# Exponential per head on ScalarE, and the PSUM banks dealt out anew, in chunk attention with a gated and a plain MLP

## The chip, the cores and the metric

The kernel runs on one core of a Trainium2 chip. The metric is the time of one execution on the device in microseconds; the time of a kernel is the median of several runs.

## The reference

Three parts follow one another, all in float32, for 8 batches of 576 rows of 512 numbers (8 heads of 64).

```python
scores = scale * np.matmul(q_c, k_c.transpose(0, 1, 2, 4, 3))   # chunks of 64 rows, each against itself
scores = scores - np.max(scores, axis=-1, keepdims=True)
attn = np.exp(scores)
attn = attn / (np.sum(attn, axis=-1, keepdims=True) + 1e-09)
out = np.matmul(attn, v_c)
...
gate = 1.0 / (1.0 + np.exp(-gate_pre))        # gate_pre: causal convolution of out with 5 taps
x = (gate * (out @ w_val)) @ w_out
...
xn = (x - mu) / np.sqrt(var + 1e-06) * g_ln
result = x + np.maximum(xn @ w_ch1, 0.0) @ w_ch2
```

## The kernel before, in words

The 4608 rows are cut into 18 **units** of 256 rows and 9 **blocks** of 512 rows, so two units make a block. Three stages follow one another.

*Attention and gate.* `slot(u)` writes the program of a unit. `a3(u)` multiplies queries by keys into the PSUM tile `sc` (two banks: 2 x 8 x 64 columns), VectorE takes the maximum of each 64 scores (L167) and subtracts it while it copies `sc` to the SBUF tile `ex` (L170), ScalarE takes the exponential of the whole `ex`, 1024 columns, in place (L174), VectorE sums (L176), inverts (L177) and scales into `pr` (L179). `a4(u)` turns `pr` on TensorE into the PSUM tile `pst` (L186, two banks) and ScalarE copies it to `pT` (L188). `a5(u)` multiplies by the values into the PSUM tile `x` (L219, two banks); ScalarE copies `x` to `xf` (L233) and, rounded, to `xh` (L236), VectorE keeps the rest in `xl` (L238). `a4` and `a5` run one unit behind `a3` (`LAG`). For each block, `conv` (L248 on ScalarE, four times L250 on VectorE per slice, into `cg`), `sigm` (L257) and four `val` chains of 12 matmuls (`psv`, L264) make the gated product: VectorE reads `psv` times `cg` into `gv` (L282), ScalarE rounds it to `gh` (L285), VectorE keeps the rest in `gl` (L286). Four `proj` chains of 12 matmuls (`pso`, also L264) follow, which ScalarE copies out (L299) and stores (L300). Between these, `split` decodes the 64-bit weights of the later stages (L87 to L90, L95, L96).

*First block of the plain MLP* (`ff1`, `ff2`), then *the other eight blocks*, two at a time (`ff_pair`).

The 8 PSUM banks of the first stage are: two for chains (pool `ps_d`, one bank a tile), two for `sc`, two for `x`, two for `pst` (pool `ps_p`).

A tile scheduler orders the instructions of each engine when the kernel is built, from dependences, priorities and costs; `tc.high_priority()` moves a group ahead. TensorE's order follows the source where `manual_schedule` is open: up to unit 4 (`MANUAL`), and again from the MLP on. Each engine then runs its list in order and waits for semaphores, and the SyncE queue holds the loads.

```python
kt, qt = t[:, 0], t[:, 1]
sc = ps_s.tile([P, 2, NG, CH], F32, tag="sc", name="sc")
```

Of the kernel before, what the change touches and what calls it, by code (L numbers as in the profile page):

```python
# [8 lines left out]
F32 = mybir.dt.float32  # L9
F32R = mybir.dt.float32r  # L10
U32 = mybir.dt.uint32
ACTF = mybir.ActivationFunctionType
ALU = mybir.AluOpType
AX = mybir.AxisListType
PSUM = bass.MemoryType.PSUM
# [4 lines left out]
def tile_chunk_attention_gated_mlp(ctx: ExitStack, tc: tile.TileContext, qk, v, w_val, conv_w, w_out, g_ln, w1, w2, out):  # L20
    nc = tc.nc
    B, S, DM = out.shape
# [39 lines left out]
    pA = s_a.enter_context(tc.tile_pool(name="pA", bufs=2, side="right"))  # L62
    ps_s = s_a.enter_context(tc.tile_pool(name="ps_s", bufs=1, space=PSUM))
    ps_x = s_a.enter_context(tc.tile_pool(name="ps_x", bufs=1, space=PSUM))
    ps_p = s_a.enter_context(tc.tile_pool(name="ps_p", bufs=1, space=PSUM))

    a_dram = [dram.tile([P, DM], F32, name=f"ad{f}") for f in range(NF)]
    w1c = [dram.tile([P, 2, 2, 2 * P], F32, name=f"wc{i}") for i in range(NF * 7 // 4)]
# [83 lines left out]
    def a3(u):  # L152
        t = qkr.pop(u)
        kt, qt = t[:, 0], t[:, 1]
        sc = ps_s.tile([P, 2, NG, CH], F32, tag="sc", name="sc")
        for g in range(NG):
            n, hp = divmod(g, NP)
            for c in range(2):
                cs = slice(n * P + c * CH, n * P + (c + 1) * CH)
                for par in range(2):  # L160
                    r0 = CH * par
                    nc.tensor.matmul(
                        out=sc[CH * c:CH * c + CH, par, g, :], lhsT=qt[r0:r0 + CH, hp, cs], rhs=kt[r0:r0 + CH, hp, cs],
                        start=True, stop=True,
                    )
        mx = pA.tile([P, 2, NG], F32, tag="mx", name="mx")
        nc.vector.tensor_reduce(out=mx, in_=sc, op=ALU.max, axis=AX.X)  # L167
        whole = exps[u % len(exps)]
        ex = whole[:, :, :, 0:CH]
        nc.vector.tensor_tensor(  # L170
            out=ex.rearrange("p g r k -> p r g k"), in0=sc,
            in1=mx.unsqueeze(3).to_broadcast([P, 2, NG, CH]), op=ALU.subtract,
        )
        nc.scalar.activation(out=ex, in_=ex, func=ACTF.Exp, scale=scale)  # L174
        sm = pA.tile([P, NG, 2], F32, tag="sm", name="sm")
        nc.vector.tensor_reduce(out=sm, in_=whole, op=ALU.add, axis=AX.X)  # L176
        nc.vector.reciprocal(out=sm, in_=sm)  # L177
        pr = pt[u] = pA.tile([P, NG, 2, CH], F32, tag="pr", name="pr")
        nc.vector.tensor_tensor(out=pr, in0=ex, in1=sm.unsqueeze(3).to_broadcast([P, NG, 2, CH]), op=ALU.mult)  # L179

    def a4(u):
        pr = pt.pop(u)
        t = pA.tile([P, NG, P], F32, tag="pT", name="pT", bufs=1)
        ps = ps_p.tile([P, NG, P], F32, tag="p", name="pst")
        for g in range(NG):
            nc.tensor.transpose(out=ps[:, g, :], in_=pr[:, g].rearrange("p r k -> p (r k)"), identity=ident)  # L186
        with tc.high_priority():
            nc.scalar.activation(out=t, in_=ps, func=ACTF.Copy)  # L188
            pT[u] = t
# [71 lines left out]
    def chain(ps, ops):  # L261
        n = len(ops)
        for i, (lt, rh) in enumerate(ops):
            nc.tensor.matmul(out=ps, lhsT=lt, rhs=rh, start=(i == 0), stop=(i == n - 1))  # L264

    def val(j, f):
        hs, ls = wv["vs"]
        fs = slice(f * P, (f + 1) * P)
        if j == NB - 1:
            ps = p2["acc"].tile([P, BLK], F32, tag=f"acc{f}", name="psv")  # L270
        else:
            ps = ps_d.tile([P, BLK], F32, tag="d", name="psv")
        ops = []
        for c in range(CT):
            ops += [(hs[c][:, fs], xh[j][:, c, :]), (hs[c][:, fs], xl[j][:, c, :]), (ls[c][:, fs], xh[j][:, c, :])]
        chain(ps, ops)
        o = boundary(j)
        gv = pD2.tile([P, BLK], F32, tag="gv", name="gv")
        with tc.high_priority():
            for lo, hi, sh in ((0, o, 0), (o, BLK, HALO)):  # L280
                if lo < hi:
                    nc.vector.tensor_tensor(out=gv[:, lo:hi], in0=ps[:, lo:hi], in1=cg[:, f, lo + sh:hi + sh], op=ALU.mult)  # L282
            a = pD1.tile([P, BLK], F32R, tag=f"gh{f}", name="gh")
            b = pD1.tile([P, BLK], F32R, tag=f"gl{f}", name="gl")
            nc.scalar.activation(out=a, in_=gv, func=ACTF.Copy)  # L285
            nc.vector.tensor_tensor(out=b, in0=gv, in1=a, op=ALU.subtract)  # L286
        gh[j, f], gl[j, f] = a, b

    def proj(j, t):
        hs, ls = wv["os"]  # L290
        ts = slice(t * P, (t + 1) * P)
        ps = ps_d.tile([P, DM], F32, tag="d", name="pso")
        ops = []
        for f in range(CT):
            ops += [(gh[j, f][:, ts], hs[f]), (gh[j, f][:, ts], ls[f]), (gl[j, f][:, ts], hs[f])]
        chain(ps, ops)
        y = pD2.tile([P, DM], F32, tag="y", name="y")
        with tc.high_priority():
            nc.scalar.activation(out=y, in_=ps, func=ACTF.Copy)  # L299
            nc.scalar.dma_start(out=y_dram[j][ts, :], in_=y)  # L300
# [343 lines left out]
    def taps():  # L644
        cwr = stg.tile([KC * CT, P], F32, tag="da", bufs=3, name="cwr")
        decode(cwu, cwr)
        ps = ps_p.tile([P, NP * P], F32, tag="p", name="pst")
        nc.tensor.transpose(out=ps[:, 0:KC * CT], in_=cwr, identity=ident[0:KC * CT, 0:KC * CT])
        nc.tensor.transpose(out=ps[:, KC * CT:(KC + 1) * CT], in_=gr, identity=ident[0:CT, 0:CT])
        nc.vector.tensor_copy(out=cw, in_=ps[:, 0:(KC + 1) * CT])  # L650
# [150 lines left out]
```

## Time and profile before

| | us |
|---|---|
| median of three runs | 1138.32 (1137.65 to 1139.07) |
| the profiled execution, its own time | 1135.95 |
| its span in the trace | 1134.2 |
| time around the span | 1.75 |
| busy: TensorE / VectorE / ScalarE / GpSimd | 1070.5 / 712.8 / 483.5 / 110.6 |
| mean granted TensorE clock | 0.977 of full speed |

The page gives busy time of each engine over the whole span; the stages differ, so the rows further down are read by stretch. A matmul's recorded duration overlaps its successor's, so for TensorE the distance from start to start counts, not the busy time. The attention and gate stage lies between 0 and about 345 us, the first MLP block up to about 455 us.

### The profile page before, as it was taken

What the parts mean: (1) busy time and instruction counts of PE and PEld (TensorE: products, weight loads), DVE (VectorE), ACT (ScalarE), POOL (GpSimd) and SP (SyncE); (2) the same over time, 40 slices, a digit from 0 to 9 for tenths busy, and PEclk for the clock granted to TensorE, in tenths of its full rate; (3) what the DMA queues carried; (4) which work ended last, traced back from release to release, by engine and by line L of the source; (5) the groups of instructions that cost most, each with busy time, mean ns of one, the idle gap of its engine ahead of it and who ended that gap; (6) DMA issues with size and microseconds to landing.
All of it is one profiled execution on the core that took longest, in us unless ns stands there. A gap on an engine that the chain in (4) does not pass through costs nothing.

```text
span 1134.2 us, 17091 instructions
## 1 busy us (share of the span) xinstructions
PE 1070.5 (94%) x6862; PEld 871.4 (77%) x6862; DVE 712.8 (63%) x1171; ACT 483.5 (43%) x832; POOL 110.6 (10%) x120
## 2 busy tenths in 40 slices
PE   5788989899898989899999999999999999999998
PEld 5676767777786868688888888888888888878877
DVE  6999999888967877545647434447444437432434
ACT  3566666566574754434444123333223333221221
POOL 2021001000003443322210000000000000000000
PEclk9799999999999999999999999999999999999999
DMA  8535546531135753634342733332733222622212
GB/s 334 169 121 166 187 133 213 179 107 72 46 120 188 225 165 119 236 118 145 126 141 100 232 99 106 112 106 89 232 105 103 99 93 89 227 93 93 75 38 75
DMA packets 58581, 155.28 MB, mean 137 GB/s; under 512 B 5742, under 2 KB 13958, under 8 KB 56198
## 3 DMA queue, kind: packets, MB, share of 16 engines
q1 hardware_dynamic: 53318, 144.75, 37.7%
q10 hardware_dynamic: 5184, 9.44, 2.2%
q8 instruction: 54, 0.88, 0.3%
q14 instruction: 25, 0.20, 0.1%
HBM read 116.41 MB, written 37.75 MB: 136 GB/s over the span
## 4 chain that ended last, share of the span: by engine, by line
PE 65%; DVE 24%; issue 4%; ACT 3%; DMA 3%; POOL 0%; SPq 0%; ACTq 0%; POOLq 0%; DVEq 0%
PE acc L499 16%; PE x L525 15%; PE psf L499 14%; PE zy L525 10%; DVE cg L250 7%; PE psv L264 5%; DVE da L89 2%; DVE da L90 2%; DVE sm L176 2%; PE acc L385 1%; DVE xl L238 1%; DMA raw<-in_moe_w_ch 1%; DVE h L537 1%; PE psh L264 1%; DVE mx L167 1%
## 5 line engine op out<-in xcount | busy, mean ns | idle before, releaser
L545 DVE TENSOR_TENSOR c<-x,c 128x512 f32<-128x512 f32 x96 | 66.2, 690 | 237.3 <-ACT c L541 181.1
L499 PE MATMUL psf<-w,h 128*128 128x512 f32 x768 | 186.0, 391 | 0.0
L499 PE MATMUL acc<-w,h 128*128 128x512 f32 x768 | 186.0, 391 | 0.0
L499 PEld LDWEIGHTS acc<-w,h 128*128 128x128 f32 x768 | 144.2, 188 | 31.4
L499 PEld LDWEIGHTS psf<-w,h 128*128 128x128 f32 x768 | 144.2, 188 | 31.4
L525 PE MATMUL x<-t,wc 128*128 128x512 f32 x576 | 148.2, 393 | 3.4 <-DVE c L545 3.4
L541 ACT ACTIVATE c<-zy 128x512 f32<-128x512 f32 x96 | 58.0, 604 | 188.4 <-PE zy L525 188.3
L525 PEld LDWEIGHTS x<-t,wc 128*128 128x128 f32 x576 | 108.8, 189 | 27.8 <-DVE c L545 4.6
L536 ACT ACTIVATE h<-c 128x512 fp32r<-128x512 f32 x96 | 60.5, 631 | 136.1 <-DVE c L545 135.5
L250 DVE SCALAR_TENSOR_TENSOR cg<-xf,cw,cg 128x516 f32<-128x516 f32 (+1 forms) x176 | 108.6, 661 | 0.0
L504 DVE TENSOR_TENSOR yt<-psf,yt 128x512 f32<-128x512 f32 x128 | 88.2, 691 | 25.0 <-PE psf L499 21.1
L525 PE MATMUL zy<-b,wc 128*128 128x512 f32 x384 | 98.9, 393 | 0.0
L525 PEld LDWEIGHTS zy<-b,wc 128*128 128x128 f32 x384 | 71.2, 188 | 14.6
L537 DVE SCALAR_TENSOR_TENSOR h<-c,h 128x512 fp32r<-128x512 f32 x96 | 68.5, 713 | 14.0 <-ACT h L536 13.9
L264 PE MATMUL psv<-xh,vh 128*128 128x512 f32 x144 | 62.1, 432 | 15.5 <-DVE gv L282 15.5
L96 POOL TENSOR_TENSOR w<-da,w 128x512 fp32r<-128x512 f32 x32 | 48.6, 1526 | 128.8 <-ACT w L95 125.6
L264 PE MATMUL psv<-xh,vl 128*128 128x512 f32 x144 | 59.6, 414 | 0.0
L264 PE MATMUL psv<-xl,vh 128*128 128x512 f32 x144 | 59.6, 414 | 0.0
L264 PE MATMUL pso<-oh,gh 128*128 128x512 f32 x144 | 58.5, 406 | 0.1
L264 PE MATMUL pso<-oh,gl 128*128 128x512 f32 x144 | 56.5, 393 | 0.4 <-DVE gl L286 0.4
L264 PE MATMUL pso<-ol,gh 128*128 128x512 f32 x144 | 56.1, 390 | 0.0
L393 POOL TENSOR_TENSOR wc<-raws,wc 128x256 fp32r<-128x256 f32 x56 | 45.3, 831 | 107.4 <-ACT wc L392 100.5
(108 smaller groups left out, 1563.3 us busy)
## 6 DMA issues: line engine op xcount, KB each, us to landing
wc<-wc SPq DMA_DIRECT2D x112, 512.0 KB, 3.2
qkr<-in_qk SPq DMA_DIRECT2D x18, 1024.0 KB, 5.9
raw<-in_moe_w_ch SPq DMA_DIRECT2D x32, 512.0 KB, 4.2
vr<-in_v SPq DMA_DIRECT2D x18, 512.0 KB, 4.2
yd<-y ACTq DMA_DIRECT2D x36, 256.0 KB, 2.8
out<-yt SPq DMA_DIRECT2D x36, 256.0 KB, 3.7
yr<-yd SPq DMA_DIRECT2D x32, 256.0 KB, 3.2
yt<-yd SPq DMA_DIRECT2D x32, 256.0 KB, 4.1
```

The lines of the kernel that those rows point to most:

```text
L89: nc.vector.scalar_tensor_tensor(out=au, in0=hw, scalar=0x80000000, in1=au, op0=ALU.bitwise_and, op1=ALU.bitwise_or)
L96: nc.gpsimd.tensor_tensor(out=lo, in0=a, in1=hi, op=ALU.subtract)
L250: nc.vector.scalar_tensor_tensor(out=o, in0=x[:, f, i + lo:i + hi], scalar=cw[:, i * CT + f:i * CT + f + 1], in1=o, op0=ALU.mult, op1=ALU.add,
L264: nc.tensor.matmul(out=ps, lhsT=lt, rhs=rh, start=(i == 0), stop=(i == n - 1))
L393: eng.tensor_tensor(out=lo, in0=a, in1=hi, op=ALU.subtract)
L499: nc.tensor.matmul(out=ps, lhsT=lt, rhs=rh, start=(g == 0 and k == 0 and (first or half)), stop=(g == 1 and k == 2 and (last or half)),)
L504: nc.vector.tensor_tensor(out=yt[i], in0=ps, in1=yt[i], op=ALU.add)
L525: nc.tensor.matmul(out=ps, lhsT=lt, rhs=rh, start=(start and c == 0 and i == 0), stop=(c == 1 and i == 2), skip_group_check=True)
L536: nc.scalar.activation(out=t[:, 0, :], in_=src, func=ACTF.Relu)
L537: nc.vector.scalar_tensor_tensor(out=t[:, 1, :], in0=src, scalar=0.0, in1=t[:, 0, :], op0=ALU.max, op1=ALU.subtract)
L541: nc.scalar.activation(out=t, in_=zy, func=ACTF.Copy)
L545: nc.vector.tensor_tensor(out=t, in0=x, in1=t, op=ALU.add)
```

## The change

Four things are edited.

1. In `a3`, VectorE no longer subtracts the maximum. It multiplies the small tile `mx` (16 numbers a partition) by `-scale`, and ScalarE reads `sc` from PSUM in 16 instructions of 64 columns, each with its column of `mx` as bias, and writes `ex`. The sum, the inverse and the product on VectorE stay. `sc` is now read until the last of the 16 exponentials, where it was read until the subtraction.
2. `pst` and `x` share one PSUM tile (tag `x`, two banks, one buffer).
3. The two banks so freed are the pool `ps_e` (two buffers of one bank). The chains of `val` and `proj` take a bank from `ps_d` and from `ps_e` by turns, through `ps_chain`, until the stage is closed; so four chains have banks.
4. The transposed taps use a tile of `ps_e`.

```diff
-    ps_p = s_a.enter_context(tc.tile_pool(name="ps_p", bufs=1, space=PSUM))
+    ps_e = s_a.enter_context(tc.tile_pool(name="ps_e", bufs=2, space=PSUM))
...
-        nc.vector.tensor_tensor(
-            out=ex.rearrange("p g r k -> p r g k"), in0=sc,
-            in1=mx.unsqueeze(3).to_broadcast([P, 2, NG, CH]), op=ALU.subtract,
-        )
-        nc.scalar.activation(out=ex, in_=ex, func=ACTF.Exp, scale=scale)
+        nc.vector.tensor_scalar(out=mx, in0=mx, scalar1=-scale, scalar2=None, op0=ALU.mult)
+        for r in range(2):
+            for g in range(NG):
+                nc.scalar.activation(out=ex[:, g, r, :], in_=sc[:, r, g, :], func=ACTF.Exp, scale=scale, bias=mx[:, r, g:g + 1])
...
-        ps = ps_p.tile([P, NG, P], F32, tag="p", name="pst")
+        ps = ps_x.tile([P, NG, P], F32, tag="x", name="pst")
...
+    chains = 0
+
+    def ps_chain(name):
+        nonlocal chains
+        chains += 1
+        pool = ps_d if chains % 2 or "acc" in p2 else ps_e
+        return pool.tile([P, BLK], F32, tag="d", name=name)
+
...
-            ps = ps_d.tile([P, BLK], F32, tag="d", name="psv")
+            ps = ps_chain("psv")
...
-        ps = ps_d.tile([P, DM], F32, tag="d", name="pso")
+        ps = ps_chain("pso")
...
-        ps = ps_p.tile([P, NP * P], F32, tag="p", name="pst")
+        ps = ps_e.tile([P, BLK], F32, tag="d", name="pst")
```

The scheduler makes another order of it. The first place is ScalarE's list in the first unit of block 3, from the turned probabilities to the copies of `x`. `ex_143` is one of the two `ex` buffers, `da` a decoded weight, and lines after the edit are seven higher in the later functions and one lower in `a3` to `a5`. Before:

```order
L188 ACTIVATE pT<-pst 128x1024
L285 ACTIVATE gh<-gv 128x512
L174 ACT_TABLE_LOAD
L174 ACTIVATE ex_143<-ex_143 128x16x64
L285 ACTIVATE gh<-gv 128x512
L87 ACTIVATE da<-raw_3785 128x512
L233 ACTIVATE xf<-x 128x4x256
L236 ACTIVATE xh<-x 128x4x256
```

The same place in the change:

```order
L173 ACT_TABLE_LOAD
L173 ACTIVATE ex_143<-sc,mx 128x64
L187 ACTIVATE pT<-pst 128x1024
L292 ACTIVATE gh<-gv 128x512
L173 ACTIVATE ex_143<-sc,mx 128x64 x6
L292 ACTIVATE gh<-gv 128x512
L173 ACTIVATE ex_143<-sc,mx 128x64 x2
L232 ACTIVATE xf<-x 128x4x256
L235 ACTIVATE xh<-x 128x4x256
L173 ACTIVATE ex_143<-sc,mx 128x64 x5
L306 ACTIVATE y<-pso 128x512
```

The exponentials stand in pieces between the other copies: 14 of the 16 come ahead of the first copy of a `pso` chain, and 2 behind it.

The second place is VectorE's list in the same unit, from the subtraction to the sum. Before:

```order
L170 TENSOR_TENSOR ex_143<-sc,mx 128x2x8x64
L88 TENSOR_SCALAR da<-da 128x512
L286 TENSOR_TENSOR gl<-gv,gh 128x512
L89 SCALAR_TENSOR_TENSOR da<-raw_3783,da 128x512
L282 TENSOR_TENSOR gv<-psv,cg 128x192
L282 TENSOR_TENSOR gv<-psv,cg 128x320
L90 SCALAR_TENSOR_TENSOR da<-raw_3783,da 128x512
L176 TENSOR_REDUCE sm<-ex_143 128x16
```

In the change, from the scaling of `mx` to the sum:

```order
L170 TENSOR_SCALAR mx<-mx 128x16
L90 SCALAR_TENSOR_TENSOR da<-raw_3744,da 128x512
L293 TENSOR_TENSOR gl<-gv,gh 128x512 x2
L289 TENSOR_TENSOR gv<-psv,cg 128x192
L289 TENSOR_TENSOR gv<-psv,cg 128x320
L89 SCALAR_TENSOR_TENSOR da<-raw_3746,da 128x512
L90 SCALAR_TENSOR_TENSOR da<-raw_3746,da 128x512
L289 TENSOR_TENSOR gv<-psv,cg 128x192
L289 TENSOR_TENSOR gv<-psv,cg 128x320
L293 TENSOR_TENSOR gl<-gv,gh 128x512 x2
L237 TENSOR_TENSOR xl<-x,xh 128x4x256
L175 TENSOR_REDUCE sm<-ex_143 128x16
```

More of VectorE's other work now stands between the maximum and the sum, the remainder `xl` of the unit before among it. On TensorE, the scores, the transposes and the product with the values of a unit have 12 or 24 chain matmuls between them in every unit from 4 to 16, where before the transposes of every second unit came straight behind the scores.

## Rows read from the trace of the kernel before

**Rows 1.** The page, VectorE's busy share in tenths, 40 slices of 28.4 us.

```profile
DVE  6999999888967877545647434447444437432434
```

**Rows 2.** Stretches: length, busy us of PE, PEld, DVE, ACT, POOL; then clock.

```profile
46.00:117.00 71.00, 57.85 (x713) 46.24 (x703) 68.97 (x105) 45.72 (x63) 10.52 (x10) 0.90 0.42 135
117.00:150.60 33.60, 31.30 (x373) 24.65 (x372) 29.68 (x46) 21.09 (x28) 3.57 (x4) 0.95 0.50 168
150.60:186.30 35.70, 30.61 (x373) 24.72 (x372) 34.57 (x52) 23.30 (x31) 4.95 (x5) 0.90 0.56 191
186.30:219.80 33.50, 30.52 (x373) 24.59 (x372) 30.58 (x47) 20.26 (x27) 0.81 (x2) 0.95 0.54 173
219.80:252.60 32.80, 30.58 (x369) 24.58 (x368) 27.73 (x42) 19.67 (x25) 0.81 (x2) 0.95 0.38 128
252.60:283.90 31.30, 29.02 (x369) 23.49 (x368) 27.68 (x42) 19.14 (x25) 0.64 (x1) 1.00 0.24 82
```

**Rows 3.** The chain of waits from 235 us: start, length, what.

```profile
235.33 1.94 ACT cg L257
...
237.29 1.16 DVE gv L282 x3
...
238.58 7.36 PE psv L264 x24
```

**Rows 4.** Waits from 46 to 345 us: total, times, longest.

```profile
PE psv L264 <- DVE gv L282: 15.5, 6, 5.1
...
PE x L219 <- ACT pT L188: 10.6, 5, 3.2
```

**Rows 5.** Groups by line and shape: busy us, mean ns.

```profile
L170 DVE TENSOR_TENSOR ex<-sc,mx 128x1024 f32<-128x1024 f32 x18 | 21.8, 1213 | 0.0
L174 ACT ACTIVATE ex<-ex 128x1024 f32<-128x1024 f32 x18 | 19.1, 1060 | 14.3 <-DVE ex L170 14.2
L177 DVE RECIPROCAL sm<-sm 128x16 f32<-128x16 f32 x18 | 4.4, 244 | 0.0
L238 DVE TENSOR_TENSOR xl<-x,xh 128x1024 fp32r<-128x1024 f32 x12 | 14.6, 1216 | 1.9 <-ACT xh L236 1.9
L335 DVE TENSOR_TENSOR w<-w,ve 128x2 f32<-128x2 f32 x16 | 2.5, 158 | 0.4
L329 DVE TENSOR_SCALAR ve<-mv 128x2 f32<-128x2 f32 x16 | 4.3, 272 | 0.1
```

**Rows 6.** Groups again: ScalarE reading PSUM, and its table load.

```profile
L188 ACT ACTIVATE pT<-pst 128x1024 f32<-128x1024 f32 x18 | 18.3, 1019 | 18.7 <-PE pst L186 18.3 <-ACT y L299 0.4
L233 ACT ACTIVATE xf<-x 128x512 f32<-128x512 f32 x4 | 2.2, 590 | 0.4 <-ACT y L299 0.4
L350 ACT ACTIVATE xt<-pst,cw 128x128 f32<-128x128 f32 x144 | 39.3, 387 | 0.0
L174 ACT ACT_TABLE_LOAD x7 | 9.0, 1283 | 0.1
```

**Rows 7.** ScalarE's timeline at 334 and 214 us: start, length of the merged run.

```profile
333.66 2.16 ACT L350 ACTIVATE xt<-pst,cw 128x128 f32<-128x128 f32 x8
...
214.43 1.07 ACT L233 ACTIVATE xf<-x 128x256 f32<-128x256 f32 x2
```

**Rows 8.** The chain of waits around 310 us: matmuls back to back.

```profile
308.59 0.85 PE x L219 x46
309.44 11.11 PE pso L264 x48
```

**Rows 9.** TensorE's timeline at 234 us: start, length, work, idle before it.

```profile
234.18 1.16 PE L162 MATMUL sc<-qkr 64*64 64x64 f32 x64
235.27 1.09 PE L186 MATMUL pst<-ident,pr 128*128 128x128 f32 x8
238.58 0.47 PE L264 MATMUL psv<-xh,vh 128*128 128x512 f32 x1 [2.22 <-DVE gv L282]
```

**Rows 10.** One more stretch, columns as in rows 2.

```profile
238.50:246.00 7.50, 7.42 (x32) 5.70 (x36) 4.46 (x8) 4.10 (x5) 0.00 (x0) 0.77 0.14 59
```

## The prediction

> **What bounds the kernel now.** I read the page's slices first, then the stretches, then the chain of waits. The change touches the attention and gate stage alone, so the reader is to ask what is full there. VectorE's line stands at 8 or 9 tenths up to the tenth slice, and at about half of that afterwards [rows 1]. By stretches [rows 2]: from 46 to 219.8 us (units 3 to 12, five blocks of work, counted by their score products) VectorE is busy 68.97 + 29.68 + 34.57 + 30.58 = 163.8 us of 173.8, 94%. ScalarE is busy 110.4 us in the same time. So here VectorE's list is the bound, and what is taken from it is worth its own length.
>
> From 219.8 to 283.9 us (two blocks, units 13 to 16) the weight decoding has run out, VectorE is busy 27.7 us of each block, and a second limit shows. The chain of waits goes from the sigmoid on ScalarE to VectorE's `gv`, from there to 24 chain matmuls of TensorE, and from these back to VectorE [rows 3]. TensorE has two banks for chains. The third `psv` chain needs the bank that `gv` reads, and `gv` needs the sigmoid. TensorE stands idle 2.22 us for it [rows 9], and 15.5 us in six such waits in the stage [rows 4]. After the wait at 236 us the granted clock is 0.77 over the next 7.5 us [rows 10], so part of it ran at the lower of the two levels (1.2 and 2.4 GHz), after an idle stretch; the 24 matmuls took 7.36 us [rows 3], where 24 at 11.11/48 = 0.231 us would take 5.5 [rows 8]. The wait costs 2.2 + 1.8 = 4.0 us in this block.
>
> **The change part by part.**
>
> *VectorE, per unit.* A subtraction of 1.213 us goes [rows 5]. A scaling of 128x16 comes. The inverse has just this shape and takes 0.244 us; the bounds are 0.158 and 0.272 us from the smallest neighbours. I take 0.244. It saves 0.97 us a unit, and sum, inverse and product stay.
>
> *ScalarE, per unit.* One exponential of 1.06 us goes [rows 5] and 16 of 64 columns come, from PSUM, with a column of `mx` as operand. No row has that. From above: a 128-column read of PSUM with such an operand (as scale) lasts 0.387 us [rows 6]; if they did not overlap, 16 x 0.387 = 6.2 us. From below: the copy of `x` that is split in two (256 and 768 columns, no such operand) takes 1.07 us [rows 7] where one of 1024 takes about 1.02 [rows 6], so 1.02 + 15 x 0.05 = 1.8 us. Nearest is the run of eight with such an operand, 2.16 us [rows 7]: (2.16 - 0.387)/7 = 0.253 us from start to start. Columns cost (1019 - 590)/512 = 0.84 ns each [rows 6], so 64 fewer make it 0.20 us, and 16 of them 3.2 us. ScalarE gets 2.1 us more a unit, 4.3 a block. It is busy (21.09 + 23.30 + 20.26 + 19.67 + 19.14)/5 = 20.7 us of blocks of 33.4 us [rows 2]; 25.0 us still fits, and idle ScalarE covers it.
>
> The Trainium skill (ScalarE: Activation LUTs, What ACT_TABLE_LOAD costs) gives 280 ns plus 0.833 ns a column for an activation with a pointer as bias, 93 ns of it overlapped: an estimate of 240 ns each, 3.8 us a unit. By that the latency below would be 0.6 us longer a unit, and the sum at most 6 us worse over ten units; the run of eight here is a little cheaper.
>
> *Latency.* From the maximum to the sum there were 1.213 + 1.06 = 2.27 us; now 0.244 + 3.2 = 3.44, and the pieces lie between other copies. Between nothing and 1.17 us a unit can be exposed on VectorE. What covers it is in the order: between scaling and sum VectorE has two or four `gv`, the `gl`, decoding and `xl`. Not all is covered. In a block's first unit two exponentials stand behind the first copy of `pso`. After `xh` come five exponentials (1.0), the copy (0.59, as a 512-column read of PSUM [rows 6]) and two more (0.4), 2.0 us, against `xl` with 1.22 on VectorE [rows 5]: 0.8 us exposed. In the second unit seven exponentials (1.4) stand against `xl`: 0.2. I take 0.4 us a unit, which is an estimate.
>
> *Scores held longer.* `sc` is freed by the last exponential. In the order the next scores come two `proj` chains or two `val` chains later, 24 x 0.231 = 5.5 us [rows 8], against the 2.0 and 1.4 us of the tail above. Nothing, as long as ScalarE is not behind. *One tile for `pst` and `x`*: `x` needs `pT` anyway, which is the copy that frees `pst`; `pst` of the next unit comes a unit later than `x`, whose readers are done in some 3 us. Nothing. *Taps*: once, nothing. Table loads (1.283 us, seven for the exponential [rows 6]) stay seven. No load on SP's queue or step of POOL is moved.
>
> *Four banks for chains.* In the blocks with decoding VectorE works during TensorE's wait, and nothing is won. In the two late ones the floor becomes TensorE: 96 x 0.231 = 22.2 us of chains, and twice scores 1.09 (from start to start), transposes 1.09 [rows 9] and values 64 x 0.85/46 = 1.18 [rows 8], 28.9 us in all, while VectorE falls to 27.7 - 1.9 = 25.8.
>
> **The sum**, against the profiled execution's 1135.95 us:
> - units 3 to 12 on VectorE, 10 x 0.97: -9.7 (9.4 to 10.6);
> - units 13 to 16: two blocks of 64.1 us together, to 2 x 28.9 and 1 us each for hand-overs, 59.8: -4.3 (0 to 6.3);
> - the last unit, where the product with the values waits 3.2 us for `pT` [rows 4] and now has another chain in front of it: -2 (0 to 3.2);
> - exposed latency in the ten units, 10 x 0.4: +4 (0 to 11.7);
> - units 0 to 2, where little covers it: +0.7 (0 to 3.5).
>
> Together -11.3, so 1124.65 us. The median of the runs stands 2.37 us above the profiled execution, so I predict **1127.0 us**; its own range is 1118 to 1135. What follows the stage moves forward with it, since the decoding done inside the stage covers the same number of weights by the order.
>
> **The rivals.**
>
> *ScalarE becomes the bound (slower).* If the 16 pieces do not overlap, a block needs 20.7 - 2.1 + 32 x 0.387 = 31.0 us of ScalarE. Filled to 90% it lasts 34.4, against 33.4 now: +1.0 in seven blocks, and in units 0 to 2 up to 0.244 + 6.2 - 2.27 = 4.2 us each, of which I count a third: 7 + 4 = +11, **1149 us**. The point at which it decides is a piece of (0.9 x 33.4 - 18.6)/32 = 0.36 us from start to start. For it: 0.387 us is a recorded length. Against: the run of eight lies at 0.253. The Trainium skill (VectorE: DVE Perf Modes, The TRN2 errata) speaks for this rival: many small tiles pay a fixed cost each, where it advises 512 elements or more.
>
> *The saving is paid back in latency (no change).* VectorE runs its list in order; if it stands before each sum for the whole 1.17 us, in all 14 units from 3 to 16, and the late blocks win half: -9.7 - 2 - 2 + 16.4 + 0.7 = +3; with half a microsecond less per unit, -4. **1139 us**. For it: the sum stands directly behind `xl` in the order. Against: VectorE's idle time of all causes is ten microseconds in the five fullest blocks [rows 2], and more work stands between maximum and sum now.
>
> *VectorE's idle time shrinks as well (faster).* The ten idle microseconds of 46 to 219.8 us are partly waits for chains. If half of them go with the bank waits, nothing is exposed and the late blocks reach the floor: -9.7 - 5 - 6.3 - 3.2 = -24, **1114 us**. For it: 15.5 us of bank waits. Against: in the fullest block VectorE is busy 34.57 of 35.7 us [rows 2], so nothing is left to win there.
>
> **How the numbers follow.** My forecast gets 0.60, ScalarE as bound 0.13, payback 0.15, the larger gain 0.12. A difference under 0.2% (2.3 us) can't be told from none. Faster by over 0.2% are forecast, the larger gain and a quarter of payback: 0.76. Payback gives about half of its chance to no change, 0.07. Slower is the rest of it and ScalarE as bound, 0.17. The range 1112 to 1141 takes in all but that bound and the outer third of the larger gain, 0.17 together.
>
> **What would show it.** In the profile after, VectorE's busy time should be 18 x 0.97 = 17.5 us lower, ScalarE's about 38 higher; runs of eight exponentials should read about 1.7 us. The waits of `psv` for `gv` should be gone or under 3 us, and the blocks of the middle should last 31 to 32 us, the late ones 30. I am wrong if sums on VectorE wait over 10 us in total for exponentials, if TensorE waits for `sc` to be read, or if pieces start over 0.36 us apart. The prediction rests most on VectorE staying the fullest engine with its order intact.

## The result, and the profile after

The changed kernel takes 1125.67 us (median of four runs, 1124.33 to 1126.50) against 1137.99 us (four runs, 1134.46 to 1139.07) for the kernel before: ratio 0.9896, 95% interval 0.9872 to 0.992. The forecast was 1127.0 us. The time came out as predicted; the reason given for it did not, as the experiments show. The profiled execution took 1125.75 us with a span of 1123.9, so 10.3 us less span than before.

The stretches of the changed kernel, cut where units 3, 13 and 17 begin their score products and where the stage's last chain ends (columns: length, busy us of PE, PEld, DVE, ACT, POOL with instruction counts, granted clock, DMA share, GB/s):

```profile
44.90:213.40 168.50, 150.25 (x1820) 119.33 (x1820) 151.30 (x235) 130.41 (x294) 20.11 (x22) 0.93 0.48 160
213.40:275.90 62.50, 58.48 (x739) 46.60 (x739) 53.20 (x86) 48.42 (x112) 0.74 (x3) 1.00 0.37 121
275.90:334.50 58.60, 56.91 (x441) 46.35 (x440) 47.87 (x95) 41.58 (x80) 0.00 (x0) 1.00 0.30 108
```

The same stage of the kernel before, its units 3 to 12 and then the whole; units 13 to 16 are the last two rows of [rows 2], and the last unit is 283.9 to 343.8 us:

```profile
45.70:219.80 174.10, 150.56 (x1820) 120.49 (x1820) 164.10 (x247) 110.66 (x147) 19.86 (x21) 0.92 0.49 160
45.70:343.80 298.10, 266.98 (x2992) 215.40 (x2992) 265.30 (x419) 187.14 (x258) 21.31 (x24) 0.95 0.41 137
```

Units 3 to 12 went from 174.1 to 168.5 us, units 13 to 16 from 64.1 to 62.5, the last unit from 59.9 to 58.6; the start of unit 3 came 0.8 us earlier, and the rest of the program is 1.0 us shorter. That is the whole 10.3. The reader is to look at VectorE's column beside the length. In units 3 to 12 VectorE had been busy 164.1 of 174.1 us, idle 10.0. Now it is busy 151.3 of 168.5, idle 17.2. Its work shrank by 12.8 us, the stretch by 5.6.

The groups that answer to [rows 5], in the changed kernel (busy us, mean ns, then idle time of the engine just before and what ended it):

```profile
L173 ACT ACTIVATE ex<-sc,mx 128x64 f32<-128x64 f32 x288 | 69.1, 353 | 28.5 <-DVE mx L170 25.6 <-issue 2.6
L170 DVE TENSOR_SCALAR mx<-mx 128x16 f32<-128x16 f32 x18 | 2.9, 162 | 0.0
L175 DVE TENSOR_REDUCE sm<-ex 128x16 f32<-128x1040 f32 x18 | 22.1, 1230 | 10.1 <-ACT ex L173 10.1
L237 DVE TENSOR_TENSOR xl<-x,xh 128x1024 fp32r<-128x1024 f32 x12 | 14.6, 1218 | 6.2 <-ACT xh L235 6.2
L249 DVE SCALAR_TENSOR_TENSOR cg<-xf,cw,cg 128x516 f32<-128x516 f32 x112 | 86.0, 818 | 0.0
```

The scaling costs 162 ns, where 244 were assumed. The large `xl` was preceded by 1.9 us of idle time before [rows 5] and is by 6.2 now; the sum stands 10.1 us waiting for exponentials. The page has VectorE busy 697.0 us (712.8 before) and ScalarE 523.4 (483.5). Pieces recorded with 353 ns overlap; ScalarE's timeline gives the distance:

```profile
159.90 1.58 ACT L173 ACTIVATE ex<-sc,mx 128x64 f32<-128x64 f32 x7
...
176.31 1.22 ACT L173 ACTIVATE ex<-sc,mx 128x64 f32<-128x64 f32 x5
```

From start to start that is (1.58 - 0.353)/6 = 0.204 us and (1.22 - 0.353)/4 = 0.217.

The waits of the changed kernel from 46 to 345 us (total, times, longest):

```profile
DVE xl L237 <- ACT xh L235: 14.4, 11, 2.0
PE sc L162 <- ACT ex L173: 11.4, 8, 2.0
...
DVE sm L175 <- ACT ex L173: 6.5, 7, 1.2
...
DVE gl L293 <- ACT gh L292: 5.6, 11, 1.0
```

The waits of `psv` for `gv`, 15.5 us before [rows 4], are gone from the list. In their place VectorE waits for ScalarE three ways, and TensorE waits for the scores' tile to be read. In units 3 to 12 alone, from 44.9 to 213.4 us, these waits for ScalarE make up 16.6 of VectorE's 17.2 idle us:

```profile
DVE xl L237 <- ACT xh L235: 9.2, 7, 1.6
DVE sm L175 <- ACT ex L173: 5.5, 5, 1.2
DVE gl L293 <- ACT gh L292: 1.9, 4, 0.8
```

The chain of waits shows how they arise, in the first unit of block 3 (start, length, what):

```profile
166.21 1.13 DVE mx L167
...
168.30 0.49 ACT gh L292
...
169.47 1.28 ACT L173
...
171.08 0.91 ACT pT L187
172.00 0.52 ACT gh L292
172.52 0.86 ACT ex L173 x5
...
174.68 0.91 ACT xf L232
175.59 0.92 ACT xh L235
176.51 1.02 ACT ex L173 x5
177.53 0.49 ACT y L306
...
178.77 1.24 DVE sm L175
```

From 168.3 to 178.77 us the chain lies on ScalarE alone: a table load (the 1.28 us at L173), the roundings `gh`, the copies, and the pieces between them. VectorE's sum starts 11.4 us behind the end of its maximum. VectorE has other work for most of that time, and what is exposed of it are the waits above. Is this the price of the per-head exponential, and if so, where does the gain come from?

### The profile page after: what moved, and what is told of

It reads as the page before. It is cut to its first block, busy times and chain, and to the rows that moved or that the text cites. A ratio compares the mean times of both kernels' runs of the same rounds, so it can differ in the third digit from the quotient of the medians.

```text
span 1123.9 us, 17355 instructions
## 1 busy us (share of the span) xinstructions
PE 1067.5 (95%) x6862; PEld 867.6 (77%) x6862; DVE 697.0 (62%) x1171; ACT 523.4 (47%) x1102; POOL 111.0 (10%) x120
## 4 chain that ended last, share of the span: by engine, by line
PE 62%; DVE 23%; ACT 8%; issue 3%; DMA 2%; POOL 1%; SPq 0%; ACTq 0%; POOLq 0%; DVEq 0%
PE acc L506 16%; PE x L532 15%; PE psf L506 15%; PE zy L532 10%; DVE cg L249 8%; ACT ex L173 3%; PE psv L263 2%; DVE sm L175 2%; DVE pr L178 2%; DVE mx L167 2%; DVE da L90 1%; PE acc L392 1%; DVE da L89 1%; DVE h L544 1%; ACT gh L292 1%
## 5 line engine op out<-in xcount | busy, mean ns | idle before, releaser
L506 PE MATMUL acc<-w,h 128*128 128x512 f32 x768 | 187.3, 393 | 0.0
L249 DVE SCALAR_TENSOR_TENSOR cg<-xf,cw,cg 128x516 f32<-128x516 f32 (+1 forms) x176 | 114.2, 698 | 0.8 <-ACT cg L247 0.7
L173 ACT ACTIVATE ex<-sc,mx 128x64 f32<-128x64 f32 x288 | 69.1, 353 | 28.5 <-DVE mx L170 25.6
L263 PE MATMUL psv<-xh,vh 128*128 128x512 f32 x144 | 61.2, 425 | 0.0
L263 PE MATMUL pso<-oh,gh 128*128 128x512 f32 x144 | 58.9, 409 | 2.1 <-ACT gh L292 2.0
L263 PE MATMUL psv<-xl,vh 128*128 128x512 f32 x144 | 58.5, 406 | 0.0
L263 PE MATMUL psv<-xh,vl 128*128 128x512 f32 x144 | 58.1, 403 | 0.0
L543 ACT ACTIVATE h<-x 128x512 fp32r<-128x512 f32 x32 | 19.2, 600 | 81.1 <-PE x L532 81.1
L263 PE MATMUL pso<-oh,gl 128*128 128x512 f32 x144 | 56.5, 394 | 0.0
```

What stands on the lines that cost most here:

```text
L173: nc.scalar.activation(out=ex[:, g, r, :], in_=sc[:, r, g, :], func=ACTF.Exp, scale=scale, bias=mx[:, r, g:g + 1])
L249: nc.vector.scalar_tensor_tensor(out=o, in0=x[:, f, i + lo:i + hi], scalar=cw[:, i * CT + f:i * CT + f + 1], in1=o, op0=ALU.mult, op1=ALU.add,
L506: nc.tensor.matmul(out=ps, lhsT=lt, rhs=rh, start=(g == 0 and k == 0 and (first or half)), stop=(g == 1 and k == 2 and (last or half)),)
L543: nc.scalar.activation(out=t[:, 0, :], in_=src, func=ACTF.Relu)
```

## The experiments

The theories, by the letters used in the expectations. **A** is the prediction's: taking the subtraction from VectorE gives most of the gain, and the banks little. **B**: the four chain banks give it, and the relief of VectorE is paid back. **A2**: what is lost of the relief is lost on ScalarE, whose list grew; more work there costs, and less (table loads too) gains. **C**: what costs is that the exponential comes in 16 pieces in ScalarE's list. **D**: the payback lies in the first unit of each block. **E**: it is that the scores are held until the last piece. **B2** sharpens B: the freed banks help because chains get them, and not a second tile for scores. Each ratio is against the kernel before, run beside that experiment; its medians were 1137.4 to 1139.2 us, so a difference of 2 us between two experiments tells little. Functions shift by a few lines from kernel to kernel, so the same operation has another line number in some rows.

### The banks alone

In the changed kernel, `a3` as it was before:

```diff
-        nc.vector.tensor_scalar(out=mx, in0=mx, scalar1=-scale, scalar2=None, op0=ALU.mult)
-        for r in range(2):
-            for g in range(NG):
-                nc.scalar.activation(out=ex[:, g, r, :], in_=sc[:, r, g, :], func=ACTF.Exp, scale=scale, bias=mx[:, r, g:g + 1])
+        nc.vector.tensor_tensor(out=ex.rearrange("p g r k -> p r g k"), in0=sc,
+            in1=mx.unsqueeze(3).to_broadcast([P, 2, NG, CH]), op=ALU.subtract)
+        nc.scalar.activation(out=ex, in_=ex, func=ACTF.Exp, scale=scale)
```

> Only the PSUM banks are dealt out anew (shared tile for transposes and attention output, four banks for chains); subtraction on VectorE and one exponential on ScalarE stay as before. Theory A, the gain comes from VectorE's relief: the bank waits of the psv chains (15.5 us in six waits before) vanish, but VectorE stays as full as before, so only the late blocks and the last unit win: 1131 to 1137 us. Theory B, the gain comes from the banks: most of the 12 us appear here, 1125 to 1129 us.

Measured: 1123.05 us, ratio 0.987 (0.9849 to 0.9891), 2 us below B's range. The banks by themselves give at least what the whole change gives. The stretches of this kernel, cut at the same units:

```profile
45.80:209.80 164.00, 149.81 (x1817) 117.51 (x1816) 162.68 (x242) 109.02 (x146) 20.76 (x21) 0.96 0.48 161
209.80:271.20 61.40, 58.92 (x741) 46.66 (x740) 58.02 (x87) 38.95 (x52) 0.89 (x3) 1.00 0.39 134
271.20:329.30 58.10, 56.87 (x441) 46.51 (x441) 45.65 (x92) 37.31 (x62) 0.00 (x0) 1.00 0.30 107
```

In units 3 to 12, where the prediction gave the banks nothing, they take 10.1 us (174.1 to 164.0). VectorE's idle time there falls from 10.0 to 1.3 us. Its waits in the kernel before, from 45 to 220 us, say what that idle time had been:

```profile
DVE gv L282 <- PE psv L264: 6.7, 6, 2.0
DVE sm L176 <- ACT ex L174: 2.4, 1, 2.4
```

6.7 of the 10.0 us were VectorE waiting for a `psv` chain. In the kernel with the banks alone no wait of `gv` for `psv` is left there, so these chains came late for want of a bank.

### The exponential alone

In the kernel before, the scaling and the 16 activations in place of the subtraction (which goes too) and the exponential; banks as before.

```diff
-        nc.scalar.activation(out=ex, in_=ex, func=ACTF.Exp, scale=scale)
+        nc.vector.tensor_scalar(out=mx, in0=mx, scalar1=-scale, scalar2=None, op0=ALU.mult)
+        for r in range(2):
+            for g in range(NG):
+                nc.scalar.activation(out=ex[:, g, r, :], in_=sc[:, r, g, :], func=ACTF.Exp, scale=scale, bias=mx[:, r, g:g + 1])
```

> Only the exponential per head, on the old banks (two for chains, two for the transposes, two for the attention output). Theory A (VectorE's relief): VectorE's busy time falls by about 16 us as in the change, the bank waits come back in the late blocks: 1126 to 1133 us. Theory B (the banks): the gain is gone and the longer exponential stands in its place, 1137 to 1145 us.

Measured: 1134.61 us, 0.9979 (0.9967 to 0.999). Its stretch of units 3 to 12, and its waits from 45 to 344 us:

```profile
45.50:221.70 176.20, 152.51 (x1816) 121.47 (x1816) 153.67 (x240) 132.60 (x297) 19.99 (x22) 0.91 0.46 156
```

```profile
DVE gv L281 <- PE psv L263: 13.0, 13, 2.4
DVE gl L285 <- ACT gh L284: 10.2, 10, 1.9
DVE xl L237 <- ACT xh L235: 8.7, 6, 1.8
```

VectorE has 10.4 us less to do in this stretch than before (164.1 over the same units), and the stretch is 2.1 us longer: idle 22.5 us. The waits for `psv` stay, and waits for ScalarE come on top. The time lies between the ranges of A (to 1133 us) and B (from 1137 us). A falls, since the relief without the banks brings 0.1 to 0.3%; B is right that the gain is gone, and wrong that the time would rise.

### Every exponential twice

```diff
-            for g in range(NG):
+            for g in [g for g in range(NG) for _ in range(2)]:
```

> The changed kernel, but each of the 16 exponentials of a unit is run twice in a row, with the same result: 16 more pieces of 0.2 us, 3.2 us more on ScalarE a unit. Theory A2, ScalarE's list is on the path in the first unit of each block (its wait chain runs table load, exponentials, copies of x, exponentials, sum): at least 3.2 us in each of nine first units and part of it in the second ones, 1150 to 1175 us. Rival, ScalarE's idle time (about 8 us a block) covers it: 1126 to 1136 us.

Measured: 1247.77 us, 1.0969 (1.0944 to 1.0994). 288 further pieces of 0.2 us are 57.6 us of ScalarE; they cost 122.1 us over the change, beyond every expectation. Unit 3 begins 29.3 us later than in the change, and the stage from there on, shown here with VectorE's waits, is 92.7 us longer:

```profile
74.20:456.50 382.30, 295.33 (x2992) 230.12 (x2992) 231.91 (x378) 275.92 (x705) 10.01 (x17) 0.86 0.28 96
```

```profile
DVE sm L175 <- ACT ex L173: 55.3, 9, 9.0
DVE xl L237 <- ACT xh L235: 46.3, 15, 7.2
DVE gv L289 <- ACT cg L256: 31.6, 8, 5.5
```

ScalarE is busy 276 of 382 us, 72%, and yet holds up everybody. So "idle ScalarE covers it" is wrong: what it had idle was not idle at the right time. With the waits the granted clock fell too, to 0.86 in the stage (0.96 over the same stage of the change), so part of the 122 us is a slower TensorE.

### Fewer table loads

The gate by `Tanh` of half the argument, which this kernel uses with 4 table loads on ScalarE where the change has 19; VectorE's `gv` takes (cg + 1) times `psv`, and the copy of `pso` the factor 0.5.

```diff
-        nc.scalar.activation(out=cg[:, :, :n], in_=cg[:, :, :n], func=ACTF.Sigmoid)
+        nc.scalar.activation(out=cg[:, :, :n], in_=cg[:, :, :n], func=ACTF.Tanh, scale=0.5)
...
-            nc.scalar.activation(out=y, in_=ps, func=ACTF.Copy)
+            nc.scalar.activation(out=y, in_=ps, func=ACTF.Copy, scale=0.5)
```

> The changed kernel, with the gate as (1 + tanh(x/2)), its factor 0.5 put into the copy of the projection: exponential and gate then need one table, and 15 of the 19 table loads of 1.28 us go, nothing else is added. Theory A2 (ScalarE's list, with one table load, is on the path in the first unit of each block): 1.3 us a block and up to 2.6, 1113 to 1119 us. Rival, VectorE alone is the bound of the middle blocks and the table loads lie in ScalarE's idle time: 1123 to 1127 us.

Measured: 1129.04 us, 0.9924 (0.9906 to 0.9942). ScalarE is busy 504.1 us instead of 523.4, and nothing is won. Its waits from 45 to 340 us:

```profile
ACT ex L173 <- DVE mx L170: 28.7, 10, 5.1
...
PE pst L185 <- DVE pr L178: 18.7, 6, 4.7
```

ScalarE now stands 28.7 us before the exponentials, waiting for maxima. VectorE's `gv` takes as long as before (443 ns against 447), so it is not what ate the gain. This part of A2 is not borne out, with a caution that holds for all these kernels: the scheduler makes a new order for each, so what fewer loads would give in the same order stays open.

### No subtraction at all

Four banks; the maximum is taken, the subtraction left out, and one exponential reads all 1024 columns from PSUM.

```diff
-        nc.vector.tensor_scalar(out=mx, in0=mx, scalar1=-scale, scalar2=None, op0=ALU.mult)
-        for r in range(2):
-            for g in range(NG):
-                nc.scalar.activation(out=ex[:, g, r, :], in_=sc[:, r, g, :], func=ACTF.Exp, scale=scale, bias=mx[:, r, g:g + 1])
+        nc.scalar.activation(out=ex.rearrange("p g r k -> p r g k"), in_=sc, func=ACTF.Exp, scale=scale)
```

> Four banks for chains; the maximum is still taken, but its subtraction is left out, and one exponential of 1024 columns reads PSUM. VectorE loses the 1.21 us a unit that the change takes from it, and ScalarE gets nothing more. Theory C, VectorE's relief is worth its own length once the banks are there, and only ScalarE's 16 pieces pay it back: 14 to 18 us under the banks alone, 1105 to 1111 us. Rival, with four banks something else than VectorE holds the stage (TensorE's floor, the order): within 5 us of the banks alone, 1118 to 1125 us.

Measured: 1108.22 us, 0.973 (0.9709 to 0.975). Two stretches and the exponential of this kernel:

```profile
43.00:201.40 158.40, 146.77 (x1822) 117.02 (x1820) 155.36 (x240) 111.36 (x149) 21.82 (x23) 0.96 0.53 177
201.40:259.00 57.60, 57.60 (x737) 46.90 (x736) 51.79 (x79) 38.66 (x50) 0.51 (x3) 1.00 0.36 120
```

```profile
L170 ACT ACTIVATE ex<-sc 128x1024 f32<-128x1024 f32 x18 | 18.6, 1035 | 27.2 <-DVE mx L167 27.1
```

With the banks, VectorE's relief is worth 14.8 us over the kernel with the banks alone, as long as ScalarE gets no more work for it. 18 x 1.21 = 21.8 us went from VectorE. Units 13 to 16 reach 57.6 us with TensorE busy for all of them.

### The pieces alone

Four banks; VectorE subtracts as before (in the place of the scaling), and the exponential runs in place in 16 pieces.

```diff
-        nc.vector.tensor_scalar(out=mx, in0=mx, scalar1=-scale, scalar2=None, op0=ALU.mult)
...
-                nc.scalar.activation(out=ex[:, g, r, :], in_=sc[:, r, g, :], func=ACTF.Exp, scale=scale, bias=mx[:, r, g:g + 1])
+                nc.scalar.activation(out=ex[:, g, r, :], in_=ex[:, g, r, :], func=ACTF.Exp, scale=scale)
```

> Four banks for chains, VectorE subtracts as before, but the exponential runs in place in 16 pieces of 64 columns. ScalarE gets some 1.5 to 2.5 us more a unit, VectorE's work is unchanged. Theory C: the pieces alone cost 10 to 20 us against the banks alone, 1133 to 1143 us. Rival, ScalarE's idle time covers them: 1122 to 1127 us.

Measured: 1125.53 us, 0.988 (0.9859 to 0.99). The pieces alone cost about 2.5 us over the banks alone, within the intervals; C asked for far more. But these pieces are shorter: read from SBUF and without a column as bias, they start 146 ns apart (median), those of the change 197 ns, so a unit's 16 take 2.3 us of ScalarE here and 3.2 there. VectorE, busy 268.67 of the 286.70 us of this stage, is seldom early enough to wait for them.

### Half of the heads each way

Four banks; the first row of chunks by subtraction and one exponential of 512 columns, the second in eight pieces with bias.

```diff
+        nc.vector.tensor_tensor(
+            out=ex[:, :, 0, :], in0=sc[:, 0], in1=mx[:, 0].unsqueeze(2).to_broadcast([P, NG, CH]), op=ALU.subtract,
+        )
+        nc.vector.tensor_scalar(out=mx[:, 1], in0=mx[:, 1], scalar1=-scale, scalar2=None, op0=ALU.mult)
+        nc.scalar.activation(out=ex[:, :, 0, :], in_=ex[:, :, 0, :], func=ACTF.Exp, scale=scale)
+        for g in range(NG):
+            nc.scalar.activation(out=ex[:, g, 1, :], in_=sc[:, 1, g, :], func=ACTF.Exp, scale=scale, bias=mx[:, 1, g:g + 1])
```

> Four banks for chains; one half of the heads (one PSUM bank of scores) keeps subtraction and one exponential of 512 columns, the other half has eight exponentials per head. VectorE is relieved of about 0.4 us a unit, ScalarE gets about 1.1 us. Theory C, cost and relief grow together: between the banks alone and the change, 1121 to 1127 us. Rival, a small load still hides on ScalarE and the relief counts: 1114 to 1119 us.

Measured: 1117.98 us, 0.9819 (0.9797 to 0.9841), better than the banks alone and than the change, and on the side of the rival to C. What the expectation calls half of the heads is one row of chunks, 8 of a partition's 16 groups. Some relief pays; with the second half of it 8 us are given back.

### The scores' tile twice, with and without the pieces

Two kernels in which the freed banks go to a second buffer of `sc`, and the chains keep two. The first has the changed kernel's exponential, the second subtraction and one exponential.

```diff
-    ps_s = s_a.enter_context(tc.tile_pool(name="ps_s", bufs=1, space=PSUM))
+    ps_s = s_a.enter_context(tc.tile_pool(name="ps_s", bufs=2, space=PSUM))
-    ps_e = s_a.enter_context(tc.tile_pool(name="ps_e", bufs=2, space=PSUM))
...
-        pool = ps_d if chains % 2 or "acc" in p2 else ps_e
+        pool = ps_d
```

> Exponential per head in every unit with two buffers of scores; the chains have two banks, transposes and attention output share a tile. To be read against the same banks with subtraction (1129.7 us). Theory E, the payback comes from scores held until the last exponential, for which TensorE waited 11 us in the change: without that wait the relief counts, 1115 to 1122 us. Theory D, the payback comes from ScalarE's list ahead of the copies of x: as with four banks it costs what it gives, 1128 to 1134 us.

> The shared tile for transposes and attention output stays and VectorE subtracts as before, but the two freed banks go to a second buffer of scores, and the chains keep two. Theory B2, it is the banks for chains that shorten the stage, because the third psv chain needn't wait for the sigmoid: the waits of psv for gv come back and the time is 1133 to 1140 us. Rival, any more freedom for the scheduler helps: 1122 to 1129 us.

Measured: 1130.85 us, 0.9931 (0.9917 to 0.9944), with the pieces; 1129.66 us, 0.9922 (0.9903 to 0.994), without. With two `sc` tiles TensorE's wait for the exponentials, 11.4 us in the change, is down to 1.4, and the pieces still bring nothing: E is not borne out. It isn't excluded for four chain banks, since the chains have two here, as in the exponential alone, where the relief brought next to nothing too; two tiles for scores and four chain banks would need ten banks. The kernel without the pieces lies 6.6 us above the one with four chain banks, and VectorE's waits show why, first in it from 44.8 to 339 us, then in the kernel before from 46 to 345 us:

```profile
DVE gv L289 <- PE psv L263: 11.4, 13, 2.4
```

```profile
DVE gv L282 <- PE psv L264: 12.6, 11, 2.1
```

So some 9 us of the gain come with the second tile for scores (with `pst` and `x` in one tile in both), and more only when chains have the banks. By the profiled execution, the longest of its six, it is 4.4 us. The time lies just above the rival's range and below B2's. These microseconds came though VectorE waited for `psv` nearly as long as before; what fell is TensorE's wait of `psv` for `gv`, from 15.5 to 4.9 us. So the waits that VectorE had for chains aren't the whole of what the banks give.

### Per head in every second unit

The change with the 16 pieces in odd units (second of a block) alone, or in even ones alone (`if u % 2 == 0:`); subtraction and one exponential in the others.

```diff
+        if u % 2:
...
+        else:
+            nc.vector.tensor_tensor(
+                out=ex.rearrange("p g r k -> p r g k"), in0=sc,
+                in1=mx.unsqueeze(3).to_broadcast([P, 2, NG, CH]), op=ALU.subtract,
+            )
+            nc.scalar.activation(out=ex, in_=ex, func=ACTF.Exp, scale=scale)
```

> Four banks for chains; the exponential per head only in the odd units (the second unit of a block's slots, where VectorE does the convolution and ScalarE has no gate to round), subtraction and one exponential in the even ones. Theory D, the payback sits in the even units, where the pieces stand between table load, gate and copies of x on ScalarE: the relief of nine odd units, 9 us, counts nearly in full, 1113 to 1117 us. Rival, the payback is the same in every unit: half of the way from the banks alone to the change, 1123 to 1126 us.

> The complement: exponential per head only in the even units, four banks. Theory D: all of the payback with half of the relief, 1125 to 1132 us. Rival, same in every unit: as with the odd units, 1121 to 1126 us.

Measured: odd 1119.49 us, 0.9828 (0.9814 to 0.9842); even 1138.94 us, 1.0005 (0.999 to 1.0021). The one is 3.6 us better than the banks alone, the other 15.9 us worse. The direction is D's; both times lie outside the ranges of D and of its rival. In the kernel with even units, TensorE's wait from 45 to 345 us, and ScalarE's timeline where the longest of it arises:

```profile
PE pso L270 <- ACT gh L299: 18.6, 9, 7.0
```

```profile
169.03 1.14 ACT L174 ACTIVATE ex<-sc,mx 128x64 f32<-128x64 f32 x5 [7.75 <-DVE mx L171]
170.03 1.05 ACT L194 ACTIVATE pT<-pst 128x1024 f32<-128x1024 f32 x1
...
172.81 1.92 ACT L263 ACTIVATE cg<-cg 128x2064 f32<-128x2064 f32 x1
...
178.06 1.16 ACT L299 ACTIVATE gh<-gv 128x512 fp32r<-128x512 f32 x2
```

Here the order put seven pieces, `pT` and a table load ahead of the block's sigmoid (L263), and a second table load, a piece and the copies of `x` between the sigmoid and the `gh`, for which a chain of TensorE waited 7.0 us. ScalarE's wait of 7.75 us for the scaled maximum isn't what that chain paid for, since the last step of the block's convolution, which the sigmoid needs, starts on VectorE only at 170.46 us. But -3.6 and +15.9 do not add to the +2.6 of all units. Since each variant has an order of its own, the size by unit isn't settled, nor how much of the 15.9 us the pieces themselves cost and how much the order around them.

### One maximum a partition, one exponential

Four banks; VectorE takes one maximum for all 1024 scores of a partition, scales it, and one exponential reads PSUM with it as bias. What the expectation calls 16 heads are a partition's 16 groups of 64 scores, 8 heads in two rows of chunks.

```diff
-        nc.vector.tensor_reduce(out=mx, in_=sc, op=ALU.max, axis=AX.X)
+        nc.vector.tensor_reduce(out=mx, in_=sc, op=ALU.max, axis=AX.XYZ)
...
-        for r in range(2):
-            for g in range(NG):
-                nc.scalar.activation(out=ex[:, g, r, :], in_=sc[:, r, g, :], func=ACTF.Exp, scale=scale, bias=mx[:, r, g:g + 1])
+        nc.scalar.activation(out=ex.rearrange("p g r k -> p r g k"), in_=sc, func=ACTF.Exp, scale=scale, bias=mx[:, 0:1])
```

> Four banks for chains; one maximum per row over all 16 heads of the tile in place of one per head, scaled on VectorE and used as the single bias of one exponential of 1024 columns from PSUM. The softmax is the same for any shift of a row; what changes is the weight of the 1e-9 in the divisor and the range that the shift guards: a head whose scores all lie far below the row's maximum is guarded less. Theory C (VectorE's relief counts in full if ScalarE gets no pieces): as without subtraction, 1107 to 1112 us. Rival, reading PSUM longer or the new order pays it back as in the change: 1118 to 1126 us.

Measured: 1111.62 us, 0.9769 (0.9748 to 0.9791), where C put it, and below both kernels. The stretch of units 3 to 12, and the new exponential:

```profile
41.70:204.10 162.40, 147.66 (x1818) 118.03 (x1817) 156.10 (x248) 111.35 (x149) 21.77 (x22) 0.95 0.51 172
```

```profile
L171 ACT ACTIVATE ex<-sc,mx 128x1024 f32<-128x1024 f32 x18 | 20.2, 1124 | 11.6 <-DVE mx L170 11.4
```

Over the whole stage VectorE is busy 252.4 us, as in the change, and ScalarE 187.3 us, as in the kernel before (187.1). VectorE idles 6.3 us in units 3 to 12 where the change has 17.2. So the relief is good, and what spends it is what comes with the 16 pieces: 33 us more of ScalarE in the stage (220.4 against 187.1), and their places between its other work. No kernel here gave ScalarE the same time in one instruction, so the two are not told apart.

Units 3 to 12 of six kernels side by side, from the rows above (idle is length less busy), and where the stage's last chain ends, in us from the start:

| kernel | length | VectorE busy | VectorE idle | stage ends |
|---|---|---|---|---|
| before | 174.1 | 164.1 | 10.0 | 343.8 |
| exponential alone | 176.2 | 153.7 | 22.5 | 343.3 |
| banks alone | 164.0 | 162.7 | 1.3 | 329.3 |
| the change | 168.5 | 151.3 | 17.2 | 334.5 |
| one maximum a partition | 162.4 | 156.1 | 6.3 | 320.4 |
| no subtraction | 158.4 | 155.4 | 3.0 | 315.3 |

Units cut by their score products do not hold the same work in each kernel: with one maximum VectorE does 4.8 us more in them than in the change, though the same 252.4 us over the stage. So the last column is the safer one to compare.

## Why the prediction was right in the time and wrong in the reason

- **Units 3 to 12.** Forecast -9.7 of relief and +4 of latency, -5.7; measured -5.6. The agreement is by accident. The step that failed is "In the blocks with decoding VectorE works during TensorE's wait, and nothing is won." The banks alone win 10.1 us there. The prediction read TensorE's waits for a bank [rows 4] and asked whether VectorE was busy meanwhile; it didn't ask VectorE's own waits, of which 6.7 us were for `psv`. It set the 10 idle us aside because of one block that was full. The third rival had the mechanism, with half of the size and in addition to the relief. The reading of [rows 1] is loose too: VectorE's line falls to about half from the seventeenth slice on, and stands at 6 to 9 in the six slices behind the tenth; nothing in the sum rests on it.
- **Exposed latency.** Forecast +4 (0 to 11.7). Between the kernel with the banks alone and the change VectorE loses 162.7 - 151.3 = 11.4 us of work and gains 17.2 - 1.3 = 15.9 us of idle time in these units, so the latency is beyond the upper bound and the per-head exponential costs 4.5 us net there. Over the stage from unit 3 on it is 14.0 us less work against 20.1 us more idle time. The bound counted only the way from the maximum to the sum. The waits show `xl`, `gl` and TensorE's scores as well: whatever else waits for ScalarE's list.
- **Units 13 to 16.** Forecast -4.3, measured -1.6; the banks alone give -2.7. The floor of 2 x 28.9 = 57.8 us was read rightly, as the kernel without subtraction reaches 57.6, but the change isn't there: with the pieces it holds 62.5. The waits of `psv` for `gv` did go, as forecast.
- **The last unit.** Forecast -2, measured -1.3. The wait for `pT`, 3.1 us in this unit (the 3.2 of [rows 4] belongs to another), is gone. **Units 0 to 2**: forecast +0.7, measured -0.8.
- **Scores held longer.** "Nothing, as long as ScalarE is not behind." TensorE waited 11.4 us for the exponentials in eight waits of the stage, and 5.0 us more just before unit 3. The text had named that as what would show it wrong. With a second tile, and two chain banks, the wait goes and the pieces bring nothing all the same, which speaks for a symptom of a late ScalarE; with four chain banks it wasn't tested.
- **The piece.** Forecast 0.20 us from start to start, measured 0.204 and 0.217 in the two runs shown, 0.197 as the median of all neighbours, well below the 0.36 at which ScalarE as bound was to decide. The estimate of 240 ns from the Trainium skill (ScalarE: Activation LUTs, What ACT_TABLE_LOAD costs) is over both; by it the pieces would have taken 0.4 to 0.6 us more a unit than these rows give. ScalarE is busy 220 of the 290 us of the stage: it is not the bound by its sum of work, as argued, though its list came late enough to hold up the others.
- **Busy times.** VectorE -15.8 us for a forecast of -17.5, though the scaling was cheaper than assumed (18.9 us of groups went): 5.6 us came back in the convolution steps, 80.4 to 86.0 us, of which more below, and 2.2 went in the decoding. ScalarE +39.9 for a forecast of +38.
- **What was to show it wrong.** Sums waited 10.1 us for exponentials over the whole span, on the line of 10, and TensorE waited for `sc`. Both marks pointed to the truth though the time did not.
- **The second rival**, saving paid back in latency, was right about the exponential: by itself it gives 0.9979. With the banks the change lies 2.6 us above the banks alone; their intervals overlap, so it is shown that it adds next to nothing to them, and not that it costs something.

Shown are: that the banks suffice for the gain; that VectorE's relief is worth 11 to 15 us when it comes without pieces; that doubling ScalarE's pieces costs twice their length, the slower clock included; that in these kernels neither fewer table loads nor, with two chain banks, a second tile for the scores brought the loss back. That the loss comes from the place of the pieces in ScalarE's in-order list rests on the chain and the waits, and on the two kernels with one exponential from PSUM. How much of it is the place, how much the longer work on ScalarE, and how much the order that the scheduler happened to make stays open, since no kernel here had the pieces moved within the same order or the same time spent in one instruction.

## What to carry to other kernels

Before a relief is credited at its length, list what the relieved engine waits for, and who waits for the engine that takes the work over: an engine that runs its list in order delays others by where a piece stands, at 72 to 76% busy already. A wait of one engine for a buffer may be paid by another: read the waits of the fullest engine, also where it is 94% busy. And an edit of two independent parts is two edits; here the half that was expected to do little did it all, and one maximum a partition (1111.62 us), which guards a group of scores far below that maximum less, or half of the groups by subtraction and half in pieces (1117.98 us), where each group needs its own maximum, is better than either kernel.

## What the runs showed of the hardware that was not expected

GpSimd's subtraction of 128x512 slows VectorE's convolution steps that run beside it. VectorE and GpSimd in the changed kernel's timeline, beside each other, and VectorE later where GpSimd does nothing:

```profile
182.28 3.17 POOL L96 TENSOR_TENSOR w<-da,w 128x512 fp32r<-128x512 f32 x2 [6.43 <-ACT w L95]
...
182.51 4.83 DVE L249 SCALAR_TENSOR_TENSOR cg<-xf,cw,cg 128x516 f32<-128x516 f32 x4
...
217.10 2.75 DVE L249 SCALAR_TENSOR_TENSOR cg<-xf,cw,cg 128x516 f32<-128x516 f32 x4
```

Four steps take 4.83 us in the one place and 2.75 in the other. In the first, the two that run beside GpSimd last 1.79 and 1.78 us, the other two 0.74 each. It is so throughout the changed kernel: of its 112 steps of 128x516, the 8 that meet a GpSimd subtraction last 1.78 us in the mean and none of the other 104 over 0.76. The new order let the convolution meet it more often, 8 times where it was 3, and the decoding less: the mean of a step went from 760 to 818 ns, while the decoding steps L89 and L90 fell from 791 to 751 and from 847 to 834 ns. The relief of an engine can so be given back by another order of the same work.

The Trainium skill (SBUF — State Buffer, SBUF: two separate sides) says that a VectorE operation with two SBUF inputs and a GpSimd operation that reads SBUF hold their shared ports in turn, each for a whole instruction. The row agrees in kind: beside 3.17 us of GpSimd, VectorE lost 4.83 - 2.75 = 2.1 us. Which instruction blocked which, no row here shows.

A column as bias adds 1124 - 1035 = 89 ns to an exponential of 1024 columns read from PSUM, by the two single exponentials above.
